# An attention and gated-MLP kernel: the first MLP product of batch 0 is split by pairs of heads, and the early pairs get offsets of their own

## The chip, the cores and the metric

The kernel runs on one core of one Trainium2 chip. Its time is the device time of one execution in microseconds (us). A run of several executions is given by its median. A profile is one execution taken by the hardware profiler; its rows count microseconds from the first instruction. The engines are called TensorE (PE in the rows; PEld is its loading of weights), VectorE (DVE), ScalarE (ACT), GpSimd (POOL) and SyncE (SP, here only a queue of transfers).

## The reference

Eight batches, eight heads, 576 positions, 64 columns per head. All in float32:

```python
q_rot, k_rot = rotate(q), rotate(k)                   # rotary embedding
scores = scale * q_rot @ k_rot.T                      # per head, 576 x 576
attn = exp(scores - max) / (sum + 1e-09)
x = (attn @ v) with the heads side by side            # 576 x 512 per batch
h = maximum(x @ w_in, 0)                              # 512 -> 1024
u, v = h[..., :512], h[..., 512:]
v_n = (v - mean(v)) / sqrt(var(v) + 1e-6)
v_s = einsum('ts,bsd->btd', w_spatial, v_n) + b_spatial[:, None]
out = (u * v_s) @ w_out                               # 512 -> 512
```

## The kernel before

Work goes by pairs of heads: pair i is two heads of batch i // 4, 32 pairs in all. For a pair, `prepare` loads q and k, multiplies them with the rotary table and adds (tiles st, on GpSimd and in part on VectorE or TensorE), and splits the results in a high part that TensorE takes at full rate and a low remainder (hq and lq for q, lk for k). From pair 4 on the parts are copied by transfers into qs, ks and qz, of which there is one each. `attention` makes nine tiles of scores (sc; tile 8 serves both heads and stands fifth), and for each the negative maximum (nmx, VectorE), the exponential (e, ScalarE) and a transposed copy (tu, VectorE); then the product with v (pv, in three chunks), and `normalise` (x, with a high and a low part). Scores have two PSUM slots, so a score waits for the exponential two scores back.

After four pairs `mlp` does the batch's MLP: pa (the half of w_in that is normalised, 5 tiles of rows, each a contraction over the four pairs' x), pb (the other half), pc (the spatial product) and pd (w_out). Each is a sum of three products of high and low parts: high by high, low by high, high by low. `norm` makes vn out of pa (vv, statistics sm, a high part on ScalarE and a remainder on GpSimd). The weights are decoded early (wi, wo: instructions on VectorE, ScalarE and GpSimd), and the spatial weights split (wsp).

Nothing is issued in the order of the code. Every operation is put into a list with a key, and `Program.run` plays the whole kernel through with its own costs and issues, for each engine, the ready operation with the lowest key whose buffers are free. Keys are 20 per pair and 80 per batch plus offsets (the tables PREP, STAGE, NORM, DEC, K at the head of the file), so a table's number moves operations before or behind others. On the chip each engine runs its list strictly in order. Where TensorE would have nothing ready early in the kernel, `run` issues warm matmuls: products of zeros of 256 columns into a free PSUM buffer.

In `rows`, the first pa of a batch waits for x of all four pairs, high and low:

```python
ahead = [*[(x[n], j) for n in range(4) for j in range(2)], *[f"wi1{n}" for n in range(4)]] if d == 0 else []
```

Of the kernel before, what the change touches and what calls it, by code (L numbers as in the profile page):

```python
# [22 lines left out]
HF = DFF // 2  # L23
# [17 lines left out]
MOE_START, MOE_LENGTH = 94.478379, 78.548222  # L41
DEC_V = [97.949631, 82.361107, 593.702782, 288.768656]
DEC_S = [84.682668, 152.53349, 99.527247]
DEC_U = [-568.813081, -65.866382, -0.431134, 175.381419]
DEC_ON = -60.279479
# [5 lines left out]
K_V = [27.234326, 64.747493]  # L51
DEC_O = [113.18323, -246.5008, -70.36556, -68.947851]
# [19 lines left out]
EARLY = -540.962515  # L72
STEAL = 253.677474
WARM_FROM, WARM_FULL, WARM_TO, WARM_NS, WARM_AFTER, WARM_COLS = 2500, 44958.22, 200000, 125, -0.15, 256
PATIENT = (DVE, ACT, POOL)
K_LATE = 163.209501
UNTIL = -5282.532269
LATE_LOAD = 300
SOON = 108.92456
FIRST = 6  # L80
PREP = [-848.367164, -374.753764, -69.9844, -244.721214, -617.60192, -1064.500205, 581.882473, -475.784363]
PREP_E = [51.687636, 298.661164, 17.879536, 140.254064, -184.884171, 639.680467, 73.636456, 484.33577]
PREP_AT = [-441.032351, -69.597063, -819.530327, -30.251418, -111.190708, 107.347515]
STAGE = [-7.255147, 1.255075, -127.272341, -353.119135, 244.349862, 3.682899, 10.320485]
STAGE_E = [-17.885167, 1.413295, -324.778667, -335.590414, -18.444203, 500.740646, 14.840595]
ATT_AT = [-7.442792, -9.232278, -6.449832, 1.846545, -111.323694, -67.478676]
NORM = [-413.12016, 513.410815, -713.32848, 231.181969, -280.547004]
NORM_E = [-178.78421, 267.172514, -208.498036, -240.944501, -239.600932]
MOE0 = [106.701094, 81.129356]
K_NORM, K_RELU, K_GATE, K_GHI, K_GLO, K_OB, K_OUT = 249.262822, 5.067081, 431.336369, -272.695754, 347.344605, 449.209189, 337.36198  # L90
# [216 lines left out]
def tile_attention_gated_mlp(  # L307
# [132 lines left out]
    def decode(key, where, at, src, after=()):  # L440

        n = f"w{'io'[where is wout]}" + "".join(map(str, at))
        tiles = {}
# [666 lines left out]
```

## Time and profile before

| | |
|---|---|
| median of 3 runs | 897.56 us (893.99 to 898.61) |
| the profiled execution | 891.51 us, its span 889.7 us |
| mean granted TensorE clock | 0.992 |
| TensorE busy | 858.7 us, 97% of the span |
| VectorE, ScalarE, GpSimd busy | 580.6, 497.5, 511.2 us |
| TensorE's share of the chain that ended last | 65%, of it warm matmuls 4% of the span |

A busy TensorE is not one that does useful work: warm matmuls count as busy. A wait is shown with the row of the instruction that ended it, as the idle time before it and the instruction (or transfer) that came last before it started.

### The profile page before, as it was taken

To read this page: it belongs to the slowest core of one execution; us is meant where nothing else is said; L and a number is where in the kernel's file an instruction comes from. 1 tells how busy PE (TensorE), PEld (TensorE's weight loads), DVE (VectorE), ACT (ScalarE), POOL (GpSimd) and SP (SyncE) were. 2 spreads that over 40 slices of the span, in tenths; PEclk is the share of its full clock that TensorE was granted. 3 is DMA by queue.
4 is the path that set the end of the run, shared out by engine and by line. 5 is a ranking of instruction groups with operands and counts; after the bars stand their busy time and mean duration, and the time that the engine had idled before them with its cause. 6 is when DMAs were issued, how large, how long until landed. Compare 5 with 4: busy or idle time off the path is not lost.

```text
span 889.7 us, 32677 instructions
## 1 busy us (share of the span) xinstructions
PE 858.7 (97%) x13709; PEld 757.9 (85%) x13709; DVE 580.6 (65%) x1169; ACT 497.5 (56%) x1239; POOL 511.2 (57%) x509
## 2 busy tenths in 40 slices
PE   9999989988999999999999999999999999999998
PEld 7666668878878998889979988899978998899898
DVE  6787788747577665857678565857687665855120
ACT  2665578635448545754558445755567555753442
POOL 7666699766357665566457664566557664312121
PEclk9998899999999999999999999999999999999999
DMA  9977646778888888877888788878987888552101
GB/s 195 246 231 188 146 104 150 174 166 190 211 175 187 189 182 213 190 175 173 210 204 193 171 179 211 186 173 187 224 200 176 187 197 205 121 115 53 54 1 55
DMA packets 99622, 150.88 MB, mean 170 GB/s; under 512 B 30929, under 2 KB 46929, under 8 KB 99474
## 3 DMA queue, kind: packets, MB, share of 16 engines
q1 hardware_dynamic: 98962, 148.12, 71.6%
q8 instruction: 108, 1.77, 0.9%
q10 hardware_dynamic: 512, 0.66, 0.3%
q14 instruction: 40, 0.33, 0.1%
HBM read 94.24 MB, written 9.88 MB: 117 GB/s over the span
## 4 chain that ended last, share of the span: by engine, by line
PE 65%; DMA 11%; issue 9%; SPq 4%; DVE 4%; POOL 4%; ACT 2%; POOLq 0%; DVEq 0%; ACTq 0%
PE sc L750 15%; PE pv L715 11%; PE pc L915 11%; PE pb L897 9%; PE pa L874 7%; PE pd L935 5%; DMA st<-in_qk_dram 4%; PE warm L1009 4%; SPq L429 3%; DMA ks<-st 2%; POOL st L563 2%; PE pr L616 1%; DMA vr<-in_v_dram 1%; DVE tu L771 1%; DVE nmx L760 1%
## 5 line engine op out<-in xcount | busy, mean ns | idle before, releaser
L760 DVE TENSOR_REDUCE nmx<-sc 128x1 f32<-128x576 f32 x288 | 211.5, 740 | 133.5 <-PE sc L750 131.2
L761 ACT ACTIVATE e<-sc,nmx 128x576 f32<-128x576 f32 x288 | 212.5, 739 | 144.7 <-DVE nmx L760 142.5
L771 DVE STREAM_TRANSPOSE tu<-e 128x576 f32<-128x576 f32 x288 | 216.5, 762 | 17.7 <-ACT e L761 9.7
L563 POOL TENSOR_TENSOR st<-st,tab 128x576 f32<-128x576 f32 x112 | 157.8, 1429 | 58.2 <-DMA st<-in_qk_dram 43.5
L715 PE MATMUL pv<-tu,vr 32*64 32x144 f32 x9216 | 177.4, 288 | 11.2 <-issue 11.2
L715 PEld LDWEIGHTS pv<-tu,vr 32*64 32x64 f32 x9216 | 147.9, 131 | 35.8 <-issue 31.8
L750 PE MATMUL sc<-ks,qs 128*128 128x288 f32 x560 | 120.9, 305 | 10.8 <-DVE rb L826 4.3
L915 PE MATMUL pc<-wsp,vn 128*128 128x288 f32 x768 | 126.2, 299 | 0.0
L874 PE MATMUL pa<-wi,x 128*128 128x512 f32 x448 | 118.6, 396 | 0.2 <-DVE rb L825 0.2
L897 PE MATMUL pb<-x,wi 128*128 128x288 f32 x768 | 117.5, 297 | 0.9 <-ACT vv L973 0.8
L935 PE MATMUL pd<-g,wo 128*128 128x288 f32 x744 | 113.6, 297 | 0.0
L915 PEld LDWEIGHTS pc<-wsp,vn 128*128 128x128 f32 x768 | 109.6, 189 | 3.6 <-issue 3.6
L750 PEld LDWEIGHTS sc<-ks,qs 128*128 128x128 f32 x560 | 88.9, 189 | 27.3 <-ACT e L761 8.8
L897 PEld LDWEIGHTS pb<-x,wi 128*128 128x128 f32 x768 | 107.0, 188 | 5.2 <-issue 2.6
L750 PE MATMUL sc<-lk,qz 128*128 128x288 f32 x504 | 108.3, 296 | 0.4 <-issue 0.4
L435 POOL TENSOR_TENSOR vn<-vv,vn 128x512 fp32r<-128x512 f32 (+1 forms) x40 | 51.4, 1292 | 98.9 <-ACT vn L432 98.6
L935 PEld LDWEIGHTS pd<-g,wo 128*128 128x128 f32 x744 | 102.9, 188 | 3.8 <-issue 3.6
L435 POOL TENSOR_TENSOR x<-rb,x 128x64 fp32r<-128x64 f32 (+1 forms) x96 | 59.4, 652 | 79.9 <-ACT x L432 79.9
L874 PEld LDWEIGHTS pa<-wi,x 128*128 128x128 f32 x448 | 79.1, 188 | 14.7 <-issue 1.8
L435 POOL TENSOR_TENSOR g<-u,g 128x288 fp32r<-128x288 f32 x64 | 51.1, 804 | 58.2 <-ACT g L432 58.2
L578 POOL TENSOR_TENSOR st<-st 128x576 f32<-128x576 f32 x56 | 80.0, 1429 | 2.9
L750 PEld LDWEIGHTS sc<-lk,qz 128*128 128x128 f32 x504 | 81.1, 189 | 0.7 <-issue 0.7
(144 smaller groups left out, 897.3 us busy)
## 6 DMA issues: line engine op xcount, KB each, us to landing
vr<-in_v_dram SPq DMA_DIRECT2D x128, 320.0 KB, 7.3
st<-in_qk_dram SPq DMA_DIRECT2D x58, 288.0 KB, 4.9
ks<-st SPq DMA_DIRECT2D x112, 144.0 KB, 4.9
st<-in_qk_dram SPq DMA_DIRECT2D x58, 256.0 KB, 5.1
qs<-hq SPq DMA_DIRECT2D x56, 164.0 KB, 4.0
qs<-lq SPq DMA_DIRECT2D x56, 164.0 KB, 3.8
out_dram<-ob SPq DMA_DIRECT2D x31, 288.0 KB, 3.1
qz<-hq SPq DMA_DIRECT2D x28, 164.0 KB, 6.8
```

Source lines behind the costliest of these rows:

```text
L435: eng.tensor_tensor(out=lo, in0=src, in1=hi.bitcast(F32), op=ALU.subtract)
L563: f = lambda e: e.tensor_tensor(out=st[j][:, cols], in0=st[j][:, cols], in1=tab2[:, cols], op=ALU.mult)
L578: f = lambda e: e.tensor_tensor(out=st[j][:, :S], in0=st[j][:, :S], in1=st[j][:, S:2 * S], op=ALU.add)
L715: nc.tensor.matmul(outs[g][64 * a:64 * a + 64], lhsT=vr[rows, NQ * (at % 4) + at // 4, a, :], rhs=tu[rows, kb, Q4 * a:Q4 * a + Q4], start= ...
L750: nc.tensor.matmul(pt[:, n_c * 512:n_c * 512 + HALF], lhsT=lhsT, rhs=rhs[:, n_c * HALF:n_c * HALF + HALF], start=(n == 0), stop=(n == len( ...
L760: op(DVE, 749, key + k_max, lambda: nc.vector.tensor_reduce(out=nmx.tile, in_=tops(pt), op=ALU.max, axis=AX.XY, negate=True), r=[pt], w=[n ...
L761: op(ACT, 920, key + k_exp, lambda: nc.scalar.activation(e.tile.rearrange("p (c n) -> p c n", c=2), tops(pt), AF.Exp, bias=nmx.tile, scale ...
L771: nc.vector.transpose(out=dst, in_=src)
L874: nc.tensor.matmul(pm[:, :HF], lhsT=lhsT, rhs=win[1, d][:, j, :], start=(d == 0 and n == 0), stop=(d == 3 and n == len(todo) - 1))
L897: nc.tensor.matmul(pm[:, :HALF], lhsT=win[0, d][:, i, f * P:(f + 1) * P], rhs=x[d][:, at:at + HALF], start=(d == 0 and n == 0), stop=(d == ...
L915: nc.tensor.matmul(pm[:, :HALF], lhsT=lhsT, rhs=rhs, start=(t == 0 and n == 0), stop=(t == 4 and n == 1))
L935: nc.tensor.matmul(pm[:, :HALF], lhsT=wout[d,][:, i, m * P:(m + 1) * P], rhs=gs[d][:, at:at + HALF], start=(d == 0 and n == 0), stop=(d == ...
```

## The change

In `rows`, for batch 0 alone, the first pa no longer waits for all x but for pair 3's token "go", which its first chunk of values sets; each pa then waits for the x of its own pair. For the fourth pair the contraction is cut in two: the two products with the high part of x and w_in's high and low parts ahead, the one with the low part of x behind, in a waiting of its own. The order of the three products is now high by high, high by low, low by high, in all batches. Early pairs (0 to 5) get one table each where they shared one, the decoding of w_in and w_out gets three offsets (DEC_G) for one, the MLP of batch 0 its own seven offsets (MOE_K0). All numbers are new. `decode`, `gate` and the others change only in which table they read.

```diff
-MOE_START, MOE_LENGTH = 94.478379, 78.548222
+MOE_START, MOE_LENGTH = 94.744184, 78.284423
...
-DEC_ON = -60.279479
+DEC_G = [-57.440314, -97.226709, 110.690024]
...
-PREP_E = [51.687636, 298.661164, 17.879536, 140.254064, -184.884171, 639.680467, 73.636456, 484.33577]
+PREP_0 = [-32.849775, 182.765619, 92.530758, 79.045448, -339.24905, 965.001318, 114.863923, 396.495195]
...
+        on = DEC_G[2 if where is wout else 1 - at[0]]
...
-        K_S, K_STEP, K_MAX, K_EXP, K_TURN, K_CHUNK, K_VAL = STAGE_E if i < FIRST else STAGE
+        K_S, K_STEP, K_MAX, K_EXP, K_TURN, K_CHUNK, K_VAL = (STAGE_0, STAGE_1, STAGE_2, STAGE_3, STAGE_4, STAGE_5)[i] if i < FIRST else STAGE
...
+        K_NORM, K_RELU, K_GATE, K_GHI, K_GLO, K_OB, K_OUT = MOE_K if b else MOE_K0
...
-                ahead = [*[(x[n], j) for n in range(4) for j in range(2)], *[f"wi1{n}" for n in range(4)]] if d == 0 else []
-
-                def mul(d=d):
-                    todo = products(x[d], t)
-                    for n, (lhsT, j) in enumerate(todo):
-                        nc.tensor.matmul(pm[:, :HF], lhsT=lhsT, rhs=win[1, d][:, j, :], start=(d == 0 and n == 0), stop=(d == 3 and n == len(todo) - 1))
-
-                key = mm(pe_ns(HF) * (2 if t == 4 else 3), mul, r=[f"wi1{d}", (x[d], 0), (x[d], 1), *ahead], w=[pm], new=[pm] if d == 0 else [])
+                ahead = [*([(x[n], j) for n in range(4) for j in range(2)] if b else [("go", NP - 1)]), *[f"wi1{n}" for n in range(4)]] if d == 0 else []
+
+                todo = [0, 1] if t == 4 else [0, 2, 1]
+                split = b == 0 and d == 3 and t < 4
+                for part in [todo[:2], todo[2:]] if split else [todo]:
+
+                    def mul(d=d, part=part, end=todo[-1]):
+                        each = products(x[d], t)
+                        for n in part:
+                            lhsT, j = each[n]
+                            nc.tensor.matmul(pm[:, :HF], lhsT=lhsT, rhs=win[1, d][:, j, :], start=(d == 0 and n == 0), stop=(d == 3 and n == end))
+
+                    low = [(x[d], 1)] if not split or part[0] == 1 else []
+                    key = mm(pe_ns(HF) * len(part), mul, r=[f"wi1{d}", (x[d], 0), *low, *ahead], w=[pm], new=[pm] if d == 0 else [])
```

What this does to the orders, at the places that the prediction speaks of. Names carry the pair or batch and the tile: sc4_8 is tile 8 of pair 4's scores, pa0_1 tile 1 of batch 0's pa, x3 pair 3's x, wi10 the decoded weights of its first 128 rows.

TensorE before, from the ninth tile of pair 4's scores (sc4_8, the fifth in order) to the first pa; sixteen warm matmuls stand ahead of it, six more ahead of sc4_2, and four between sc4_4 and pa0_0:

```order
L750 MATMUL sc4_8_2064<-ks_71,qs_70 128x288 x4
L750 MATMUL sc4_8_2064<-lk4_1314,qz_72 128x288 x2
L750 MATMUL sc4_4_2074<-ks_71,qs_70 128x288 x2
L750 MATMUL sc4_4_2074<-lk4_1314,qz_72 128x288 x2
L1009 LDWEIGHTS zero_64
L1009 MATMUL warm_2081<-zero_64 128x256
```

TensorE now, from pair 4's second score to its tile 8:

```order
L767 MATMUL sc4_1_1955<-ks_71,qs_70 128x288 x2
L767 MATMUL sc4_1_1955<-lk4_1314,qz_72 128x288 x2
L897 MATMUL pa0_0_1969<-wi10_685,x0_996 128x512 x3
L897 MATMUL pa0_0_1969<-wi11_754,x1_1349 128x512 x3
L897 MATMUL pa0_0_1969<-wi12_1047,x2_1668 128x512 x3
L767 MATMUL sc4_2_2000<-ks_71,qs_70 128x288 x2
L767 MATMUL sc4_2_2000<-lk4_1314,qz_72 128x288 x2
L767 MATMUL sc4_3_2007<-ks_71,qs_70 128x288 x2
L767 MATMUL sc4_3_2007<-lk4_1314,qz_72 128x288 x2
L897 MATMUL pa0_0_1969<-wi13_954,x3_1996 128x512 x2
L897 MATMUL pa0_1_2021<-wi10_685,x0_996 128x512 x3
L897 MATMUL pa0_1_2021<-wi11_754,x1_1349 128x512 x3
```

All 26 warm matmuls between sc4_1 and pa0_0 are gone, and 17 matmuls of pa0_0 and pa0_1 stand ahead of sc4_8; the last of pa0_0, with x3's low part, stands behind sc4_8.

GpSimd before, up to the low half of q of pairs 6 and 7 (lq made out of st6_0 and st7_0):

```order
L435 TENSOR_TENSOR wo0_2515<-vlwo0_2480,wo0_2515 128x512
L435 TENSOR_TENSOR vn_1965<-vv0_2_2350,vn_1965 128x512
L563 TENSOR_TENSOR st7_1_2271<-st7_1_2271,tab2_63 128x576 x2
L435 TENSOR_TENSOR lq_74<-st6_0_1693,hq_73 128x512
L435 TENSOR_TENSOR lq_74<-st6_0_1693,hq_73 128x4x16
L578 TENSOR_TENSOR st7_1_2271<-st7_1_2271 128x576
L435 TENSOR_TENSOR lq_74<-st7_0_1971,hq_73 128x512
```

GpSimd now, at the same place:

```order
L451 TENSOR_TENSOR wo0_2506<-vlwo0_2461,wo0_2506 128x512
L580 TENSOR_TENSOR st7_1_2194<-st7_1_2194,tab2_63 128x576
L451 TENSOR_TENSOR vn_1977<-vv0_3_2209,vn_1977 128x512
L595 TENSOR_TENSOR st7_1_2194<-st7_1_2194 128x576
L451 TENSOR_TENSOR lq_74<-st6_0_1691,hq_73 128x512
L451 TENSOR_TENSOR lq_74<-st6_0_1691,hq_73 128x4x16
L451 TENSOR_TENSOR vn_1977<-vv0_4_2428,vn_1977 64x512
L451 TENSOR_TENSOR lq_74<-st7_0_1961,hq_73 128x512
```

The remainder of vn's tile 3 (of vv0_3) and the sum of st7_1 now stand ahead of pair 6's lq; that of tile 4 stands between the two lq.

ScalarE before, at pair 6's exponentials (e6_4 is that of tile 4) and the step st8_1, the high part of pair 8's k:

```order
L761 ACTIVATE e6_8_2980,sums0_66<-sc6_8_2946,nmx6_8_2971 128x576
L900 ACTIVATE u0_3_2963<-pb0_31_2916 128x288
L652 ACTIVATE st8_1_2789<-st8_1_2789 128x576
L761 ACTIVATE e6_4_3006,sums0_66<-sc6_4_2973,nmx6_4_2990 128x576
L761 ACTIVATE e6_5_3021,sums0_66<-sc6_5_2999,nmx6_5_3011 128x576
L761 ACTIVATE e6_6_3042,sums0_66<-sc6_6_3023,nmx6_6_3031 128x576
```

ScalarE now:

```order
L924 ACTIVATE u0_3_2901<-pb0_31_2851 128x288
L778 ACTIVATE e6_8_2932,sums0_66<-sc6_8_2904,nmx6_8_2917 128x576
L778 ACTIVATE e6_4_2952,sums0_66<-sc6_4_2926,nmx6_4_2937 128x576
L778 ACTIVATE e6_5_2967,sums0_66<-sc6_5_2946,nmx6_5_2958 128x576
L669 ACTIVATE st8_1_2766<-st8_1_2766 128x576
L448 ACTIVATE g0_0_2991<-u0_0_2516 128x288
L778 ACTIVATE e6_6_2994,sums0_66<-sc6_6_2969,nmx6_6_2979 128x576
```

st8_1 has moved behind the exponentials of tiles 4 and 5, and a step of g (of the gate) stands ahead of that of tile 6.

## Rows read from the trace of the kernel before

**Rows 1.** The page: busy time of each engine, share, instructions.

```profile
PE 858.7 (97%) x13709; PEld 757.9 (85%) x13709; DVE 580.6 (65%) x1169; ACT 497.5 (56%) x1239; POOL 511.2 (57%) x509
```

**Rows 2.** Stretches: length; busy PE, PEld, DVE, ACT, POOL; clock, DMA share, GB/s.

```profile
112.00:130.00 18.00, 15.56 (x262) 11.75 (x246) 15.79 (x27) 13.05 (x30) 16.48 (x17) 1.00 0.47 112
130.00:180.00 50.00, 48.04 (x827) 42.50 (x825) 41.07 (x89) 35.20 (x89) 44.97 (x41) 1.00 0.70 155
180.00:230.00 50.00, 41.74 (x779) 38.30 (x780) 27.99 (x51) 22.46 (x56) 32.86 (x31) 0.97 0.77 175
```

**Rows 3.** Timeline of TensorE, pair 4's scores: start, length, instructions.

```profile
119.53 1.91 PE L1009 MATMUL warm<-zero 128*128 128x256 bf16 x6
121.33 0.53 PE L750 MATMUL sc<-ks,qs 128*128 128x288 f32 x2
...
122.49 2.68 PE L1009 MATMUL warm<-zero 128*128 128x256 bf16 x16
124.92 0.77 PE L750 MATMUL sc<-ks,qs 128*128 128x288 f32 x4
...
126.33 0.61 PE L1009 MATMUL warm<-zero 128*128 128x256 bf16 x4
126.78 2.35 PE L874 MATMUL pa<-wi,x 128*128 128x512 f32 x9
```

**Rows 4.** Timeline of TensorE, pairs 5 to 8; in brackets idle time and releaser.

```profile
154.57 4.56 PE L897 MATMUL pb<-x,wi 128*128 128x288 f32 x33
159.06 1.22 PE L715 MATMUL pv<-tu,vr 32*64 32x144 f32 x60
...
164.24 0.51 PE L750 MATMUL sc<-ks,qs 128*128 128x288 f32 x2 [0.71 <-DMA qs<-lq]
...
168.37 0.53 PE L750 MATMUL sc<-ks,qs 128*128 128x288 f32 x2 [0.96 <-ACT e L761]
...
182.32 0.85 PE L750 MATMUL sc<-ks,qs 128*128 128x288 f32 x2 [2.35 <-ACT e L761]
...
187.49 0.42 PE L750 MATMUL sc<-ks,qs 128*128 128x288 f32 x2
...
209.45 0.43 PE L750 MATMUL sc<-ks,qs 128*128 128x288 f32 x2
...
212.70 0.50 PE L750 MATMUL sc<-ks,qs 128*128 128x288 f32 x2 [1.48 <-ACT sums L781]
```

**Rows 5.** Timeline of GpSimd around the low halves of q.

```profile
119.15 1.65 POOL L386 MEMSET vn<- 64x512 f32 x3 [1.35 <-PE pv L715]
...
158.48 1.65 POOL L435 TENSOR_TENSOR lq<-st,hq 128x512 fp32r<-128x512 f32 x2
160.00 1.50 POOL L578 TENSOR_TENSOR st<-st 128x576 f32<-128x576 f32 x1
165.05 1.57 POOL L435 TENSOR_TENSOR lq<-st,hq 128x512 fp32r<-128x512 f32 x2 [3.55 <-DMA qs<-lq]
166.64 2.62 POOL L435 TENSOR_TENSOR vn<-vv,vn 128x512 fp32r<-128x512 f32 x2
```

**Rows 6.** Timeline of VectorE: lk of pairs 6 and 7.

```profile
159.12 2.99 DVE L540 SCALAR_TENSOR_TENSOR lk<-st 128x576 fp32r<-128x576 f32 x1
...
164.32 0.76 DVE L540 SCALAR_TENSOR_TENSOR lk<-st 128x576 fp32r<-128x576 f32 x1
```

**Rows 7.** Timeline of ScalarE: st8, the exponential behind it, pair 7's last.

```profile
180.86 0.68 ACT L652 ACTIVATE st<-st 128x576 fp32r<-128x576 f32 x1 [2.97 <-POOL st L578]
181.45 0.72 ACT L761 ACTIVATE e<-sc,nmx 128x576 f32<-128x576 f32 x1
...
211.13 0.74 ACT L761 ACTIVATE e<-sc,nmx 128x576 f32<-128x576 f32 x1 [0.28 <-DVE nmx L760]
```

**Rows 8.** Stretches as in rows 2, behind the wait of 2.35.

```profile
182.00:184.00 2.00, 1.68 (x7) 1.69 (x8) 1.09 (x2) 0.99 (x4) 1.92 (x3) 0.56 1.01 224
184.00:186.00 2.00, 2.00 (x11) 2.00 (x11) 1.30 (x3) 0.83 (x2) 1.06 (x1) 0.59 0.13 34
```

More of the change, by code (lines that the diff above doesn't have):

```diff
@@ L83 @@
[L83 to L89, printed above, removed]
@@ new lines @@
+NORM = [-428.465703, 609.682147, -692.799463, 236.099243, -298.747737]
+NORM_0 = [-244.559891, 517.601008, -157.093041, -167.545156, -105.82433]
+NORM_1 = [-192.810612, 190.930437, -214.131948, -74.395379, -216.726448]
+NORM_2 = [-280.191903, 293.806751, -51.742277, -217.96091, -290.765893]
+NORM_3 = [-223.29783, 172.651756, -240.046007, -365.293658, -238.893886]
+NORM_4 = [-144.081309, 379.339015, -91.243063, -180.710848, -372.571447]
+NORM_5 = [-135.364254, 127.973129, -108.584507, -265.034273, -292.363128]
@@ L476, in decode @@
-        op(ACT, 500, key - DEC_ON, lambda: nc.scalar.activation(pt.tile, ints(), AF.Copy, bias=1.0, scale=2.0**-20), w=[pt])
-        op(DVE, 640, key - DEC_ON, lambda: stt(out=val.tile, in0=word(0, U32), scalar=2.0**-52, in1=pt.tile, op0=ALU.mult, op1=ALU.add), r=[t0, pt], w=[val], new=[val])
+        op(ACT, 600, key - on, lambda: nc.scalar.activation(ints(), ints(), AF.Relu, bias=bias, scale=float(2**23)), r=["bias"], w=[pt])
+        op(DVE, 640, key - on, lambda: stt(out=sg.tile, in0=word(1), scalar=-(2**31), in1=ints(), op0=ALU.bitwise_and, op1=ALU.bitwise_or), r=[t1, pt], w=[sg], new=[sg])
@@ L479, in product @@
+        op(DVE, 640, key - on, lambda: ts(out=ints(), in0=word(1), scalar1=0xFFFFF, scalar2=None, op0=ALU.bitwise_and), r=[t1], w=[pt])
+        op(ACT, 500, key - on, lambda: nc.scalar.activation(pt.tile, ints(), AF.Copy, bias=1.0, scale=2.0**-20), w=[pt])
+        op(DVE, 640, key - on, lambda: stt(out=val.tile, in0=word(0, U32), scalar=2.0**-52, in1=pt.tile, op0=ALU.mult, op1=ALU.add), r=[t0, pt], w=[val], new=[val])
         def product(e):
             e.tensor_tensor(out=val.tile, in0=val.tile, in1=sg.tile.bitcast(F32), op=ALU.mult)
-        prog.either({POOL: pool_ns(HF), **({DVE: 640} if key - DEC_ON < EARLY else {})}, key - DEC_ON, lambda e: product(vec[e]), r=[sg], w=[val])
@@ L483, in decode @@
-        op(ACT, 480, key - DEC_ON, high, r=[val], w=[t0, t1, (n, "hi")])
-        prog.either({POOL: pool_ns(HF), **({DVE: 640} if key - DEC_ON < EARLY else {})}, key - DEC_ON, lambda e: rest_lo(vec[e], where[at][:, 1, :], val.tile, where[at][:, 0, :]), r=[val, (n, "hi")], w=[n])
+        prog.either({POOL: pool_ns(HF), **({DVE: 640} if key - on < EARLY else {})}, key - on, lambda e: product(vec[e]), r=[sg], w=[val])
+        op(ACT, 480, key - on, high, r=[val], w=[t0, t1, (n, "hi")])
+        prog.either({POOL: pool_ns(HF), **({DVE: 640} if key - on < EARLY else {})}, key - on, lambda e: rest_lo(vec[e], where[at][:, 1, :], val.tile, where[at][:, 0, :]), r=[val, (n, "hi")], w=[n])
@@ L994, in norm, with gate @@
             op(POOL, pool_ns(HF), key, port=True, f=lambda: rest_lo(nc.gpsimd, vn(4, 0)[64:P], vv[0:64], vn(4, 0)[0:64]), r=[vv, ("vn", t, 0)], w=[("vn", t, 1)])
-    def gate(u, g, c, pm, key, done):
+    def gate(u, g, c, pm, key, done, ks):
+        K_GATE, K_GHI, K_GLO = ks
         cc = slice(c * HALF, (c + 1) * HALF)
```

53 lines of the change are left out of this document (33 added, 20 removed).

## The prediction

> **What bounds the kernel now.** I read the page first: TensorE is busy 97% of the span [rows 1], so the end moves only by what TensorE does for nothing or waits for. Then the table by stretch [rows 2], to see where that is: of the 50 us from 180 on it is busy 41.74, and in the 18 us before 130 it has 2.44 us idle, and part of the busy time there is warm matmuls on zeros, which give no result. In the stretch 130 to 180 the picture is another: VectorE 41.07, GpSimd 44.97 of 50, so a TensorE that gets ahead there may only wait longer. Third, the timeline of TensorE between the scores of pair 4 [rows 3]: three runs of warm matmuls lie there, 6, 16 and 4, after which the first MLP product starts at 126.78. Fourth, the same timeline up to pair 8 [rows 4], for the waits that come next: 0.71 ahead of pair 6's first score, 0.96 ahead of its second, 2.35 ahead of its eighth (tile 6), 1.48 ahead of pair 8's first. Last, GpSimd [rows 5], VectorE's lk [rows 6] and ScalarE [rows 7] around those waits, for what ends them, and the granted clock behind the longest [rows 8].
>
> Up to the scores of pair 3 all engines' orders are as before but for neighbours changing places, and from pair 11 on TensorE executes the same work ahead of each score again; the sum is therefore made between 104 and 230 us. After that TensorE is the bound, and I carry the shift to the end unchanged; TensorE's whole idle time is 889.7-858.7 = 31.0 us, 12.7 of it in the three stretches of [rows 2], so swaps of neighbours behind 230 have a part of the other 18.3 to win or to double, most of it early: I take 0, and 2 either way into the range.
>
> **The change part by part.**
> *The early products.* The 26 warm matmuls go. By starts in [rows 3] they hold TensorE for 121.33-119.53 = 1.80, 124.92-122.49 = 2.43 and 126.78-126.33 = 0.45, together 4.68 us. In their place stand 17 pa matmuls at 2.35/9 = 0.26 us, 4.4 us, so the scores of pair 4 stay where they are within 0.3 us and the MLP is 4.4 to 4.7 us ahead. pa's last product of tile 0 now waits for pair 3's low half from GpSimd. It stands behind the fifth score of pair 4 in order (tile 8), near 126, and one weight remainder that stood ahead of that low half is now behind it; I take no wait (bound: 0.5, as the first pa stood at 126.78 for all of x). Queued behind that matmul are only scores and the next pa, in order.
>
> *To pair 6's first score.* Before it the new order has 18 pb matmuls more. One is (159.06-154.57)/33 = 0.136 [rows 4], so 2.45 us. TensorE would come there at 164.24-0.71-4.68+2.45 = 161.3. But that score needs the low half of q, which GpSimd makes. In the order before, GpSimd makes it at 158.48 and is done at 160.00; GpSimd has no idle time between 119.15 and there (its two ends in [rows 5]). The new order puts two more operations ahead: the remainder of vn's tile 3, 2.62/2 = 1.31, and the sum of st7, 1.50. Against that GpSimd may use part of its 1.35 idle at 119.15, since the operation now first there is a decode product, whose input the order of VectorE has two instructions sooner, and not the zeroing of vn that waited for TensorE's values: between 0 and 1.35, I take 1.0, nearer the upper end, as two VectorE instructions are worth about that. So the low half is done at 160.00+1.31+1.50-1.0 = 161.81. From there to the score it took 164.24-160.00 = 4.24 (two copies on the SP queue and their landing; nothing is moved ahead of them on SP there). The score starts at 166.05, and TensorE waits 4.75 in place of 0.71. Of the lead of 4.68, only 2.45-1.81 = 0.64 is left here.
>
> *From there to pair 6's eighth score.* Before: 182.32-164.24 = 18.08, with 0.96 and 2.35 of waits, so 14.77 of work. Now 18 pb fewer and 2 pc more, -16 x 0.136 = -2.18: 12.59. The 0.96 goes because ScalarE has fewer vv and vn steps ahead of pair 6's first exponential (the vv and vn of the MLP's tile 3 are done before it). The 2.35 goes because ScalarE no longer stands at st8 (idle 2.97 until GpSimd's sum, [rows 7]) ahead of exponentials 4 and 5; st8 is now behind them. What is late next is exponentials 6 and 7 behind st8, which hold pair 7's first score. GpSimd's sum for st8 ended at 180.86 [rows 7]; it moves by the low half's 1.81, less the vn remainder that now stands ahead of the low half, 1.31, plus one st9 product that is new ahead of it, 1.5 as the sum in [rows 5]: 182.9 at the latest. With ScalarE's st8 (181.45-180.86 = 0.59), one g and the exponential, some 1.9 together, the slot is free at 184.8, just before the score wants it (185.0 below). The cost of the long wait: after the 2.35 idle the granted clock was 0.56 and 0.59, the lower level of 1.2 GHz in most of 4 us [rows 8], which cost 1.68x0.44+2.00x0.41 = 1.56 us. After 1.48 [rows 4] it did not fall: the stretch 180 to 230 as a whole has 0.97 [rows 2], which those 4 us explain. A wait of 4.75 is over 2.35, so I take the fall, 1.56; without it the gain is that much larger. Pair 6's eighth score: 166.05+12.59+1.56 = 180.20.
>
> *To pair 7's first score.* Before 187.49-182.32 = 5.17 with those 1.56 in it; now 9 pc more, 1.22: 4.83, at 185.03. By then 11 more pc are done, 1.50. Lead: 187.49-185.03+1.50 = 3.96.
>
> *To pair 8.* Four warm matmuls are new between the pc there, 4 x 2.43/16 = 0.61. Ahead of pair 8's first score, 16 pc stand behind pair 7's last (209.45) in place of 8, 1.09 us more cover for a wait of 1.48 [rows 4]. Against that the values of pair 7 now follow directly on that score, and need its last exponential (211.13 [rows 7], 1.68 behind the score, 0.74 long, and VectorE's transposed copy behind it, put at as much; TensorE has 16 x 0.136 and two scores in that time, about 3): some 0.5 us of wait. Net 0.6 gained.
>
> Sum: 3.96-0.61+0.6 = 4.0 us. The sum is against the profiled execution, 891.51 us (span 889.7), so 887.5; the median of the runs shown is 897.56, 0.7% above it, and I take the same 4.0 from it: 893.5.
>
> **A rule weighed.** VectorE's lk of pair 6 took 2.99 us at 159.12 and the next one, 164.32, 0.76 [rows 6]; GpSimd worked without a break beside the first and was idle from 161.5 to 165.05 before the second [rows 5]. The Trainium skill, SBUF — State Buffer, "Who interferes with whom", says that a VectorE instruction with two inputs in SBUF and a GpSimd instruction that reads SBUF exclude one another for a whole instruction, and that the order of issue decides who blocks. The trace agrees: lk ended when GpSimd paused. By that rule the new order, which puts a vn remainder into that pause, speaks against the change.
>
> **The rivals.**
> *Slower: GpSimd's unbroken stretch now outlasts TensorE's lead.* The place is pair 6's first score. Nothing of the 1.35 is recovered (1.0 lost against my sum), pair 7's lk also meets a busy GpSimd (2.99-0.76 = 2.23 during which VectorE takes no maximum of pair 6), and exponentials 6 and 7 stand 2.35 behind st8 as 4 and 5 did, with a second fall of the clock, 1.56. 4.0-1.0-2.23-2.35-1.56 = -3.1: 900.7. For it: GpSimd's 44.97 of 50. Against it: in the order VectorE has nothing urgent at that lk. The rule weighed above is this mechanism's. It decides from the point where pair 6's first score starts later than 164.24+2.45 = 166.7; I forecast 166.05.
> *No change: the lead is eaten at pair 6 and not given back.* If the wait at the eighth score only moves to the ninth or to pair 7, the 0.64 left at pair 6's first score less the 0.61 of warm matmuls remain: 897.5. For it: pairs 6 and 7 need VectorE and ScalarE for each score. Against it: both are busy 28.0 and 22.5 of 50 us from 180 on [rows 2].
> *All of it kept.* If the low half is not later than before (the planner has put vn's remainder where GpSimd would have waited), TensorE keeps the 4.68, loses the waits of 0.96 and 2.35 and the 1.56 of low clock, and the last two terms cancel: 9.5, or 888.0. For it: the idle 3.55 of GpSimd right behind [rows 5]. Against it: two operations stand ahead of it in the order, whatever follows.
>
> **How the numbers follow.** Mine 0.50 (890.5 to 896.0: without the fall of the clock 5.5 gained, with 1.35 recovered 0.35 more; with 0 recovered and a wait behind st8 1.5 left). All kept 0.15 (888 to 890.5). No change 0.20 (896 to 898.5). Slower 0.15 (899 to 902). The range that leaves out half of the best case and most of the slower one is 888.5 to 899. A measurement of this kernel can tell 0.5%, 4.5 us, from no change: the line lies at 893.1, inside my own case. Faster takes a little over half of mine and all of "all kept", 0.42; slower only the far end of the slower case, 0.07; within, 0.51.
>
> **What would show it.** Right: pa starts before pair 4's third score, no run of warm matmuls behind 112, a wait of 3 to 5 us ahead of pair 6's first score with a granted clock near 0.5 behind it, no wait over 1 us at pair 6's eighth score, and TensorE's busy time less by 4 to 5. Wrong: that wait under 1 us (the gain is then near 9), or the first score of pair 6 later than 166.7, or new waits over 1 us in 230 to 890, where I price nothing.

## The result, and the profile after

The kernel after takes 901.36 us (median of 15 runs, 894.84 to 909.64), the kernel before 895.2 (15 runs, 887.12 to 900.76): a ratio of 1.0091, interval 1.0065 to 1.0117. The ratios in this text are formed from the fast executions of both kernels, so they are not the quotients of the medians (1.0069 here). It is slower, where I forecast 893.5 and gave slower a chance of 0.07. The profiled executions are 904.19 us (span 902.3) and 891.51.

The page of after, first its busy row (columns as in [rows 1]), then the group with the most idle time on TensorE: busy, mean ns, then idle time and what ended most of it.

```profile
PE 860.0 (95%) x13686; PEld 761.6 (84%) x13686; DVE 578.0 (64%) x1169; ACT 498.4 (55%) x1239; POOL 513.1 (57%) x509
L767 PE MATMUL sc<-ks,qs 128*128 128x288 f32 x560 | 121.2, 306 | 20.1 <-DVE rb L843 12.4
```

The same group in the kernel before:

```profile
L750 PE MATMUL sc<-ks,qs 128*128 128x288 f32 x560 | 120.9, 305 | 10.8 <-DVE rb L826 4.3
```

TensorE's work is the same within 1.3 us [rows 1]; what grew is idle time, and most of it is scores that wait for rb, the normaliser's sums. These go by SP to DRAM and back, turned (rt, rtNd, rb), and VectorE scales a pair's values with them; a following score waits for the PSUM that this frees.

The last two stretches of [rows 2], of after, and one more, 230 to 330, with before's row of it last:

```profile
130.00:180.00 50.00, 43.19 (x788) 38.71 (x787) 37.30 (x87) 33.73 (x86) 45.40 (x41) 0.97 0.67 149
180.00:230.00 50.00, 44.84 (x817) 41.05 (x816) 34.03 (x62) 24.90 (x62) 33.25 (x32) 1.00 0.86 190
230.00:330.00 100.00, 92.53 (x1617) 83.55 (x1616) 62.29 (x133) 54.99 (x139) 56.84 (x55) 1.00 0.77 180
```

```profile
230.00:330.00 100.00, 97.30 (x1655) 88.05 (x1654) 68.45 (x143) 56.93 (x146) 58.46 (x56) 1.00 0.84 189
```

The gain at 180 to 230 (44.84 in place of 41.74 busy) is there, and it is paid back on both sides: 4.85 at 130 to 180 and 4.77 at 230 to 330. Both losses are new waits; the second lies where I priced nothing.

The lines that answer to [rows 3, 4], TensorE of after:

```profile
121.75 2.21 PE L897 MATMUL pa<-wi,x 128*128 128x512 f32 x9
...
167.06 0.50 PE L767 MATMUL sc<-ks,qs 128*128 128x288 f32 x2 [0.66 <-DMA qs<-lq]
...
175.22 0.54 PE L767 MATMUL sc<-ks,qs 128*128 128x288 f32 x2 [3.35 <-DVE rb L843]
...
190.18 0.51 PE L767 MATMUL sc<-ks,qs 128*128 128x288 f32 x2 [0.81 <-issue]
...
247.64 2.96 PE L959 MATMUL pd<-g,wo 128*128 128x288 f32 x21
...
282.57 0.77 PE L767 MATMUL sc<-ks,qs 128*128 128x288 f32 x4 [2.95 <-DVE rb L843]
```

The first product runs early, as the change says. Pair 6's first score waits 0.66, not the 4.75 that I forecast; its third score waits 3.35, for rb of pair 5. Pair 7 starts at 190.18 (185.03 forecast, 187.49 before).

To place the loss I took the start of each pair's first and last maximum on VectorE from both traces. After is behind before by 1.70 us at pair 4's first, 3.55 at pair 5's last, 2.75 at pair 6's first, 1.60 at pair 8's first, 4.97 at pair 12's last, and 12.64 at pair 31's last. The 1.70 I count as chance: TensorE's granted clock was at the lower level (0.5, 1.2 GHz) from 83.45 to 97.11 in after and from 83.24 to 93.48 in before, 3.42 us longer, of which half is lost; another profile of the same order up to there (after with more instructions, below) had 10.24 us of it. That it is chance alone is not shown: the four profiles with before's early order had 10.24 each. So in these two profiles the early part has brought 0.1 us by pair 8 in place of 4, pairs 8 to 12 cost 3.4, and the rest 7.7, of which two falls of the clock (3.41 us long each, at 609 and 711, half of that lost) are 3.4.

After's profile is a good one of its early order, as the profiles of the experiments below show. From pair 4's first maximum to pair 8's first it took 97.3 us; the nine profiles with this order there took 97.3 to 103.0 (mean 99.9), the four with before's 95.8 to 98.6 (mean 97.1). The ranges overlap, but in the mean the early part costs 2.8 us where I forecast a gain of 4.

### The profile page after: what moved, and what is told of

Read it like the earlier page. It is cut to its first block, busy times and chain, and to the rows that moved or that the text cites. A ratio compares the mean times of both kernels' runs of the same rounds, so it can differ in the third digit from the quotient of the medians.

```text
span 902.3 us, 32617 instructions
## 1 busy us (share of the span) xinstructions
PE 860.0 (95%) x13686; PEld 761.6 (84%) x13686; DVE 578.0 (64%) x1169; ACT 498.4 (55%) x1239; POOL 513.1 (57%) x509
## 4 chain that ended last, share of the span: by engine, by line
PE 63%; DMA 13%; SPq 8%; issue 6%; DVE 4%; POOL 3%; ACT 2%; ACTq 0%; DVEq 0%; POOLq 0%
PE sc L767 15%; PE pc L939 11%; PE pv L732 11%; PE pb L921 9%; PE pa L897 8%; PE pd L959 7%; SPq L445 5%; DMA st<-in_qk_dram 3%; DMA vr<-in_v_dram 2%; PE warm L1034 2%; DMA qz<-hq 1%; DVE tu L788 1%; DMA qs<-lq 1%; PE pr L633 1%; POOL st L580 1%
## 5 line engine op out<-in xcount | busy, mean ns | idle before, releaser
L732 PE MATMUL pv<-tu,vr 32*64 32x144 f32 x9216 | 179.1, 289 | 13.7 <-issue 12.9
L767 PE MATMUL sc<-ks,qs 128*128 128x288 f32 x560 | 121.2, 306 | 20.1 <-DVE rb L843 12.4
L939 PE MATMUL pc<-wsp,vn 128*128 128x288 f32 x768 | 128.3, 301 | 1.0 <-DVE nmx L777 1.0
L921 PE MATMUL pb<-x,wi 128*128 128x288 f32 x768 | 120.6, 299 | 0.3
L897 PE MATMUL pa<-wi,x 128*128 128x512 f32 x448 | 116.4, 395 | 0.0
```

The lines of the kernel that those rows point to most:

```text
L732: nc.tensor.matmul(outs[g][64 * a:64 * a + 64], lhsT=vr[rows, NQ * (at % 4) + at // 4, a, :], rhs=tu[rows, kb, Q4 * a:Q4 * a + Q4], start= ...
L767: nc.tensor.matmul(pt[:, n_c * 512:n_c * 512 + HALF], lhsT=lhsT, rhs=rhs[:, n_c * HALF:n_c * HALF + HALF], start=(n == 0), stop=(n == len( ...
L897: nc.tensor.matmul(pm[:, :HF], lhsT=lhsT, rhs=win[1, d][:, j, :], start=(d == 0 and n == 0), stop=(d == 3 and n == end))
L921: nc.tensor.matmul(pm[:, :HALF], lhsT=win[0, d][:, i, f * P:(f + 1) * P], rhs=x[d][:, at:at + HALF], start=(d == 0 and n == 0), stop=(d == ...
L939: nc.tensor.matmul(pm[:, :HALF], lhsT=lhsT, rhs=rhs, start=(t == 0 and n == 0), stop=(t == 4 and n == 1))
```

## The experiments

Before is run beside each group. Each ratio is of a kernel against before, with its 95% interval. The early theories were A (the structure itself), B (the normaliser's trip on SP), C (the count of instructions on TensorE), D (the new numbers of the tables for later pairs); later ones R (SP's order of the normaliser's fetches), W (TensorE's own order) and X (the late end of batch 0's MLP keeps x of pair 7 out, that keeps the one rb buffer, and the normalisers of pairs 8 and 9 are late).

### Structure, count and tables

**The structure alone**, in before with its own tables:

```diff
+ahead = [("go", NP - 1)] if b == 0 else [...]     # pa's waits
+for part in [[0, 2], [1]] if b == 0 and d == 3 else [...]
```

> The kernel before, with every number of its tables as it was, and only the two edits of the first MLP step: the wait for the fourth pair's value step in place of the four x tiles, and the fourth pair's multiplies in two parts. In its order, as in the kernel after, pair 9's normaliser goes out and comes back on SP behind the next pair's st loads, and 26 warm-up multiplies are gone. A, the structure costs the time by itself: 901 us (ratio to before 1.006 to 1.009). B, the place of the normaliser's round trip on SP costs it: 899 to 901, with one idle of 2 to 3 us on TensorE before pair 10's scores, released by VectorE's rb. C, the place of the instruction count against the fetched blocks costs it: anything from 892 to 901, since this kernel has its own count (52 instructions fewer than before). D, the searched tables cost it: 892 to 895, no worse than before.

902.03 us, 1.0074 (1.0046 to 1.0102). Slower by itself, and its longest wait is one that after does not have. Its rows on VectorE and on TensorE:

```profile
145.11 5.02 DVE L540 SCALAR_TENSOR_TENSOR lk<-st 128x576 fp32r<-128x576 f32 x1
151.76 0.85 PE L750 MATMUL sc<-ks,qs 128*128 128x288 f32 x2 [8.60 <-DVE rb L826]
```

lk takes 5.02 us where it took 2.99 and 0.76 [rows 6], the scaling by rb stands behind it on VectorE, and TensorE waits 8.60. GpSimd's five instructions from 142.94 to 149.52, all with inputs in SBUF, follow on one another there without a break. The Trainium skill, SBUF — State Buffer, "Who interferes with whom", says that the port pair that VectorE shares with GpSimd is an exclusive lock, and that a VectorE instruction with two SBUF inputs contends with a GpSimd instruction that reads SBUF. The trace agrees: lk ends at 150.13, 0.61 behind the last of these five. In after, with all its new tables, the same lk takes 1.95. Behind pair 8 this kernel loses as after does, with before's tables: x of pair 7 on ScalarE starts at 251.35, behind a wait of 4.12 for pd, and the score at 286.16 waits 2.31 for rb.

**After with more instructions**: 23 pa multiplies issued as two of 256 columns. **Before with fewer**: the last 46 warm matmuls as 23 of 512 columns.

```diff
-nc.tensor.matmul(pm[:, :HF], lhsT=lhsT, rhs=win[1, d][:, j, :], ...)
+for lo, hi in ((0, 256), (256, 512)):             # for 23 of them
+    nc.tensor.matmul(pm[:, lo:hi], lhsT=lhsT, rhs=win[1, d][:, j, lo:hi], ...)
```

```diff
+cols = 256 if n < 231 else 512 if n % 2 else 0    # of the n-th warm matmul
```

> The kernel after, with its order untouched, and 23 of the first multiplies of the MLP's first step (512 columns) issued as two of 256, so that from pair 7 on each of TensorE's instructions has the number that it has in the kernel before (46 instructions more than after). C, the instruction count decides where TensorE runs out of fetched instructions in the value steps: 894 to 897 us, 4 to 7 below the kernel after, idle before pv put down to issue back from 12.9 to about 11 us, and the clock falls at 609 and 711 us gone. A, B and D: 901 us as the kernel after, within 1.5.

> The kernel before, with its order untouched, and the last 46 warm-up multiplies of 256 columns issued as 23 of 512, so that each of TensorE's instructions after them has the number that it has in the kernel after (46 fewer than before). C: 899 to 901 us, ratio to before 1.004 to 1.007, idle before pv put down to issue up by 1.5 to 2 us and clock falls behind 500 us. A, B and D: as before, 895 us within 1.5 (ratio 0.998 to 1.002).

The first 907.47, 1.015 (1.0114 to 1.0186); the second 894.82, 1.0018 (0.9995 to 1.004). The count as it was before makes after no faster, and the count of after makes before no slower: C falls. The first is 6 us above after, which none of the theories said; the cause is open. The idle time put down to issue ahead of pv does move with such edits (12.9 us in after, 18.6 and 9.4 in these two, 11.2 in before), but the time doesn't follow it.

**After with before's numbers in the tables of pairs from 6 on and of the MLP from batch 1 on:**

```diff
-PREP, STAGE, NORM, MOE_START, MOE_LENGTH, K_V[1], MOE_K = (after's)
+PREP, STAGE, NORM, MOE_START, MOE_LENGTH, K_V[1], MOE_K = (before's)
```

> The kernel after, with the tables for pairs 6 to 31 and for the MLPs of batches 1 to 7 as they were before (the two edits and all early tables as after). Its order has the normalisers of pairs 8 and 9 ahead of the st loads on SP, as before. A, the structure or the early tables cost the time: 900 to 902. B, the normaliser's round trip: 896 to 898, the idle of 2.95 us before pair 10's scores gone, and no clock fall behind 500 us only by chance. C, the instruction count (48 fewer than before): 900 to 902. D, the late tables as a whole: 894 to 896.

903.63, 1.013 (1.0087 to 1.0174). It told little, since pairs 6 and 7 no longer fit the early tables: lk took 6.12 us there, again beside a GpSimd without a break, a score waited 8.23 behind it, and that covers whatever came later.

```profile
153.36 6.12 DVE L557 SCALAR_TENSOR_TENSOR lk<-st 128x576 fp32r<-128x576 f32 x1
```

### The late normalisers of pairs 8 and 9

What stands behind the 2.95 at 282.57, in after: x of pair 7 on ScalarE and GpSimd, the fetch of pair 8's rb on SP, then pair 9's, and its scaling on VectorE.

```profile
248.64 0.78 ACT L448 ACTIVATE x<-rb 128x512 fp32r<-128x512 f32 x2 [2.42 <-PE pd L959]
249.35 1.85 POOL L451 TENSOR_TENSOR x<-rb,x 128x512 fp32r<-128x512 f32 x3 [2.21 <-ACT x L448]
251.54 1.94 SPq L445 DMA_DIRECT2D rb<-rt8d  x3
274.92 1.92 SPq L445 DMA_DIRECT2D rb<-rt9d  x3
281.54 0.52 DVE L842 TENSOR_TENSOR rb<-pv,rb 128x144 f32<-128x144 f32 x2 [3.38 <-DMA rb<-rt9d]
```

And in before x of pair 7 (GpSimd's part; ScalarE's began at 241.92, not 248.64), the fetch of pair 8's rb, and its scaling:

```profile
242.62 1.84 POOL L435 TENSOR_TENSOR x<-rb,x 128x512 fp32r<-128x512 f32 x3 [15.05 <-ACT x L432]
244.49 2.74 SPq L429 DMA_DIRECT2D rb<-rt8d  x3
251.44 0.52 DVE L825 TENSOR_TENSOR rb<-pv,rb 128x144 f32<-128x144 f32 x2 [1.02 <-DMA rb<-rt8d]
```

There is one rb. It is free when x of pair 7 has been read out of it (244.46 before, 251.20 after), and rb of pair 8 is fetched then: 244.49 and 251.54. From that issue to the scaling it is 6.95 us in before (251.44 - 244.49) and 7.72 in after (at 259.26). And x of pair 7 is late because it waits for pd, w_out's product of batch 0: in after no pd stands ahead of pair 7's values and 72 of 96 ahead of pair 8's, where before has 24 and 84. The structure alone, with before's tables, has 0 and 72 as well and the same late x of pair 7 (251.35), so this comes without the new numbers.

**SP's order alone.** The fetches that stand behind other transfers in after are put ahead of them; then also pair 5's; and in before, pair 8's and 9's are held behind the loads:

```diff
+HOLD = {"st12_0": "rb8", "vr9": "rb8", "ob0_3": "rb8", "st12_1": "rt9", "st13_0": "rb9"}   # after: held until
+HOLD = {..., "st8_0": "rb5"}                                                              # after, second
+HOLD = {"rb8": "vr9", "rt9": "st12_1", "rb9": "st13_0"}                                   # before
```

> The kernel after; every engine's order as it was but SP's, where five moves change places so that they stand as in the kernel before: rb of pair 8 ahead of st12_0, vr9 and the fourth output tile, rt of pair 9 ahead of st12_1, rb of pair 9 ahead of st13_0. R, the normalisers of pairs 8 and 9 come late because SP issues other loads first: VectorE's scale of pair 8 at about 252 to 254 us in place of 259, no idle of 2.95 us before pair 10's scores, the 6 us that pairs 9 and 10 take longer than before are gone, 896 to 898 us (4 to 6 below the kernel after). W, the 6 us come from TensorE's own order there: 900 to 902, the waits only change their names.

> As the kernel with pairs 8 and 9 first, and also rb of pair 5 ahead of st8_0 (three issues of 0.6 us). R: rb of pair 5 issued 1.9 to 2 us sooner, the idle of 3.35 us before pair 6's third score 1.2 to 2 us, perhaps too short for the clock to fall (1.7 us more): 2 to 3.5 us below the kernel with pairs 8 and 9 alone, 893 to 896 us. W: 900 to 902.

> The kernel before; every engine's order as it was but SP's, where rb of pair 8 is put behind st12_0 and vr9, rt of pair 9 behind st12_1 and rb of pair 9 behind st13_0, as in the kernel after. R: VectorE's scale of pair 8 later by 4 us or more, an idle of 2 to 3 us on TensorE before pair 10's scores released by VectorE's rb, 3 to 6 us in all: 897 to 900 us, ratio to before 1.003 to 1.007. W: 894 to 895, as before.

907.33, 1.0138 (1.0094 to 1.0181); 909.66, 1.0151 (1.0103 to 1.02); 909.17, 1.0156 (1.0117 to 1.0195). R falls as a cure: ahead in the queue, the fetch holds SP until x of pair 7 leaves rb. SP's and GpSimd's rows of the first:

```profile
245.76 0.54 SPq L455 DMA_DIRECT2D out_dram<-ob  x1
...
253.39 1.85 POOL L461 TENSOR_TENSOR x<-rb,x 128x512 fp32r<-128x512 f32 x3 [2.08 <-ACT x L458]
255.27 1.92 SPq L455 DMA_DIRECT2D rb<-rt8d  x3
```

From 246.30 to 255.27 SP does nothing, and loads stand behind it. The third says that the lateness is enough by itself: in before, with the fetch at 252.03, TensorE waits 9.59 us at one place.

```profile
252.03 1.92 SPq L439 DMA_DIRECT2D rb<-rt8d  x3
...
261.33 1.62 PE L884 MATMUL pa<-wi,x 128*128 128x512 f32 x3 [9.59 <-DVE rb L835]
```

**The trip of pair 5 taken away**: `SPREAD = 5` is the first pair whose sums go by DRAM.

```diff
-SPREAD = 5
+SPREAD = 6
```

> The kernel after with pair 5's normaliser spread by TensorE, as those of pairs 0 to 4 are (one constant, 5 to 6): 32 narrow multiplies on ones in place of the trip to DRAM and back. The planner writes its order anew with it; rt and rb of pair 9 come to stand ahead of the st loads, rb of pair 8 does not. R: the idle of 3.35 us before pair 6's third score and the clock fall behind it are gone for about 0.5 us of multiplies, and the idle of 2.95 us before pair 10's scores: 4 to 8 us below the kernel after, 893 to 897 us. W: the time moves with TensorE's order, and could be 898 to 904.

905.49, 1.0113 (1.0078 to 1.0148). It is no gain: another order of the whole early part comes of it, and what it did to the wait alone can't be told.

**The cause taken away** (X against R and W): the last 12 pd of batch 0 get a key that is lower by 200.

```diff
+sooner = 200 if b == 0 and m == 3 and c == 1 else 0    # of pd's key
```

> The kernel after; the planner's key of the last output group of batch 0's MLP (12 multiplies of pd) lowered by 200. In the order all 96 multiplies of pd then stand ahead of pair 8's values on TensorE (before: 84 and 12 inside; after: 72, and 21 of the rest behind pair 9's third score), SP's rt and rb of pair 9 come to stand ahead of the st loads by themselves, and from pair 11 on all is as in the kernel after. X, the late end of that MLP keeps the slot that pair 7's x needs, x keeps the one rb buffer, and so the normalisers of pairs 8 and 9 come late: x of pair 7 on ScalarE at about 242 us in place of 248.6, the scale of pair 8 at about 252 in place of 259.3, the idle of 2.95 us before pair 10's scores gone, 4 to 6 us below the kernel after, 895 to 898 us. Y, what is lost is lost elsewhere (the late tables, pair 5): 900 to 902.

```profile
242.63 0.76 ACT L448 ACTIVATE x<-rb 128x512 fp32r<-128x512 f32 x2
...
251.65 1.91 SPq L445 DMA_DIRECT2D rb<-rt8d  x3
```

901.36, 1.0079 (1.0044 to 1.0114), beside 901.36 of after: no gain in the median. The mechanism goes most of the way: x of pair 7 is at 242.63, and the fetches of pair 9 move ahead of the loads by themselves, but rb of pair 8 is still issued at 251.65, behind a load. TensorE's waits from 230 on, in after (to 341) and here (to 340), as "engine line, what it waited for: us, times, longest":

```profile
PE pv L732 <- issue: 3.3, 3, 1.7
PE sc L767 <- DVE rb L843: 2.9, 1, 2.9
PE sc L767 <- DMA qs<-lq: 1.0, 1, 1.0
```

```profile
PE pv L732 <- issue: 1.8, 3, 1.1
PE sc L767 <- DVE rb L843: 1.6, 1, 1.6
```

7.2 has become 3.4, where before has 2.7. From pair 8's first maximum to pair 12's last it took 121.9 us, before 121.8 and after 125.1. Over the profiles: five with after's order there took 125.1 to 128.7 (mean 127.2), three with before's 121.4 to 121.8 (121.6), three with these pd ahead 121.9 to 123.8 (122.6). So after's order costs some 5.6 us there, and this edit gives 4.7 of it back.

The profile loses it again ahead of that, by three more falls of the clock (at 190, 200 and 217). Each comes with a wait of TensorE: 1.81 at pair 7's first score (189.12), 2.44 in pair 7's values (199.78, put down to issue), 2.00 at pair 8's first score (216.97). In after the same three places waited 0.81, 1.35 and 0.93, with no fall. Five of the nine profiles with this early order have falls between 189 and 225, none of the four with before's. With the late tables of before, the same edit is worth 2 to 3 us in the medians, below.

### The late tables

Before's numbers from pair 12 and batch 3 on in after; after's numbers there in before; the first with the twelve pd ahead as well:

```diff
+LATE = 12
+... = STAGE_L if i >= LATE else STAGE      # so PREP, NORM, K_V; MOE_L, MOE_KL from batch 3
```

> The kernel after up to pair 11, and from pair 12 and the third batch's MLP on with the tables of the kernel before. D, the late tables cost 3 to 5 us between pair 12 and the end (in the runs so far that stretch took 476 to 482 us in five kernels with the late tables of after, 470 to 477 in five with those of before): 896 to 899 us. X, nothing is lost there but by chance: 900 to 902.

> The kernel before up to pair 11, and from pair 12 and the third batch's MLP on with the tables of the kernel after. D: 3 to 5 us above the kernel before, 897 to 900 us, ratio 1.003 to 1.006, the stretch from pair 12 to the end 476 to 480 us. X: as before, 893 to 896.

> The kernel after with both changes: the last output group of batch 0's MLP ahead of pair 8's values, and from pair 12 on the tables of the kernel before. X and D both right: 890 to 894 us, no slower than the kernel before. X alone: 895 to 898. D alone: 896 to 899. Neither: 900 to 902.

897.49, 1.0042 (1.0011 to 1.0072); 895.28, 1.001 (0.9981 to 1.0038); 894.24, 0.9984 (0.9957 to 1.001). So taking the late tables back alone is worth 3.9 of the 6.2 us, taking back pd's late end alone nothing in the median, and the two together all of it. Whether the numbers are bad as such is open: in before they cost 0.1%, but the interval reaches 0.4%, as much as in after. From pair 12's last maximum to pair 31's last, the seven profiles with after's numbers took 475.0 to 481.9 (mean 477.8), the seven with before's 469.7 to 476.8 (mean 472.5). TensorE's waits in that stretch, before and then after:

```profile
PE sc L750 <- DVE rb L826: 4.0, 5, 1.0
PE pv L715 <- issue: 3.2, 5, 1.2
PE sc L750 <- ACT e L761: 0.5, 2, 0.3
PE sc L750 <- issue: 0.4, 1, 0.4
```

```profile
PE pv L732 <- issue: 5.7, 5, 1.8
PE sc L767 <- DVE rb L843: 5.3, 6, 1.4
PE sc L767 <- ACT e L778: 1.3, 1, 1.3
PE sc L767 <- issue: 0.7, 1, 0.7
```

No one wait carries it; the sum of many goes from 8.1 to 13.0.

**Which table**: the MLP's alone; the pairs' alone; the pairs' with the twelve pd ahead; of the pairs' only STAGE (the scores').

```diff
+MOE_L, MOE_KL from batch 3                      # first
+PREP_L, STAGE_L, NORM_L, K_V from pair 12       # second; third: and sooner = 200
+STAGE_L from pair 12                            # fourth
```

> The kernel after; from the third batch's MLP on the MLP's tables as before, those of the pairs as after. If the MLP's late tables carry the loss behind pair 12 (the groups of pb in another order, the output of the first group one place earlier on SP): 896 to 899 us as with all late tables. If those of the pairs carry it: 900 to 902.

> The kernel after; from pair 12 on the tables of the pairs (preparation, scores, normaliser) as before, those of the MLP as after. If those of the pairs carry the loss behind pair 12: 896 to 899 us. If the MLP's carry it: 900 to 902. If neither k1 nor k2 is below 900, it takes both, or the loss is not the tables'.

> The kernel after, from pair 12 on with the tables of the pairs as before, and the last output group of batch 0's MLP ahead of pair 8's values. X (the late end of that MLP costs pairs 9 and 10 what they take longer): 3 to 5 us below the kernel with the pairs' late tables alone (897.97), 893 to 895 us. If what pairs 9 and 10 give back is lost again ahead of them, as in the kernel with the last output group alone: 897 to 899.

> The kernel after, from pair 12 on with the table of the scores alone as before (when a score, its maximum, exponent and transposes are due): TensorE's order is that of the kernel with all the pairs' late tables, SP's that of the kernel after. If the order of TensorE and VectorE in the steady batches carries the loss: 897 to 899 us. If it was the loads of pairs 11 and 12 in the other order: 900 to 903.

904.6, 1.0128 (1.0082 to 1.0174); 897.97, 1.0055 (1.0024 to 1.0087); 895.73, 0.9998 (0.9973 to 1.0023); 900.1, 1.0068 (1.0037 to 1.0099). By the medians it is the pairs' tables, not the MLP's, but the profiles don't bear that out: from pair 12's last maximum to pair 31's last the first took 472.9 us, as short as with before's numbers, and the other three 471.3 to 471.8. The first lost ahead of that stretch (pair 12's last maximum starts at 349.32, in after at 340.23), where its order is that of after. So in these single profiles either table is enough to shorten the stretch, and which one the median loss hangs on stays open. The fourth has the order of the second on TensorE and VectorE and SP's of after. Its median lies between them with overlapping intervals, but its stretch (471.3) is as short as the second's (471.8): the loads of pairs 11 and 12, which change places on SP in the second, are not needed for that.

### The early wait for pair 5's normaliser

On top of the version with both undone: pair 5's fetch held ahead of a load; and 16 matmuls on zeros put into the batch's first pb of tile 3, ahead of the waiting score.

```diff
+HOLD = {"st8_0": "rb5"}
```

```diff
+for _ in range(16):
+    nc.tensor.matmul(pm[:, HALF:HALF + 224], lhsT=zero[:, :P], rhs=zero[:, :224], start=False, stop=False)
```

> The kernel with both changes (last output group ahead, late tables of before), and rb of pair 5 ahead of st8_0 on SP, nothing else moved. If the trip of pair 5's normaliser sets pair 6's third score: the wait of 2.45 us there 0.5 to 1.2 us, no clock fall at 171 us, 1 to 3 us below the kernel with both, 891 to 893 us, and so 0.2 to 0.4% below the kernel before. If it is hidden anyway (the next wait takes its place): 893 to 895.

> The kernel with both changes, and 16 warm-up multiplies of 224 columns on zeros (some 1.5 us) on TensorE ahead of pair 6's third score, where it waits 2 to 3.4 us; they add zeros to columns that nothing reads. If the clock fall behind that wait costs 1.7 us and the warm-up keeps the clock up: 1 to 2 us below the kernel with both, 892 to 893. If the fall comes anyway or is as rare as in the kernel before: 893 to 896, no gain.

896.49, 1.0026 (0.9993 to 1.0058); 898.87, 1.0045 (1.0013 to 1.0078), beside 894.24 without. First the version without, then these two:

```profile
171.12 0.85 PE L773 MATMUL sc<-ks,qs 128*128 128x288 f32 x2 [2.45 <-DVE rb L849]
...
186.86 0.51 PE L773 MATMUL sc<-ks,qs 128*128 128x288 f32 x2 [1.62 <-ACT g L454]
```

```profile
171.59 0.53 PE L783 MATMUL sc<-ks,qs 128*128 128x288 f32 x2 [1.15 <-DVE rb L859]
...
189.26 0.64 PE L783 MATMUL sc<-ks,qs 128*128 128x288 f32 x2 [5.04 <-DMA qs<-lq]
```

```profile
175.18 0.53 PE L773 MATMUL sc<-ks,qs 128*128 128x288 f32 x2 [0.84 <-DVE rb L849]
...
190.68 0.51 PE L773 MATMUL sc<-ks,qs 128*128 128x288 f32 x2 [2.86 <-DMA qs<-lq]
```

In the first the wait is halved, in the second it is covered, and in neither does a fall of the clock follow it. Pair 7's first score then waits for its own q, 5.04 and 2.86: what TensorE gained it lost to the preparation of q.

No version was measurably faster than before: the two best lie at 0.9984 and 0.9998.

## Why the prediction was wrong

*The products fit in place of the warm matmuls: right.* pa runs at 0.25 us each (2.21/9), ahead of pair 4's tile 8, and no wait came there; GpSimd's order didn't hold it.

*"The score starts at 166.05, and TensorE waits 4.75 in place of 0.71": wrong on TensorE's side.* The score started at 167.06, so q came 1.0 late to my forecast. But TensorE came at 167.06 - 0.66 = 166.40 and not at 161.3. Of these 5.1, 1.7 is the early clock and 2.5 are new waits between 121 and 166, a stretch that I took to be without them (0.9 I can't place):

```profile
PE sc L767 <- ACT e L778: 2.0, 2, 1.3
PE pv L732 <- ACT vv L997: 0.8, 1, 0.8
```

against 0.3 in before. TensorE had the multiplies, but ScalarE had not made the exponentials sooner.

*"The 0.96 goes ... the 2.35 goes": right, but a wait that I didn't see takes their place.* Between the start of pair 5's values and pair 6's third score, before had 30 multiplies of pb and after has 15; with the wait of 0.96, which is gone, they were the cover of pair 5's trip through DRAM. That trip in after, on VectorE and SP:

```profile
161.89 0.15 DVE L854 STREAM_TRANSPOSE rt<-sums 128x32 f32<-128x32 f32 x1
162.25 1.95 DVE L557 SCALAR_TENSOR_TENSOR lk<-st 128x576 fp32r<-128x576 f32 x1
174.28 0.52 DVE L842 TENSOR_TENSOR rb<-pv,rb 128x144 f32<-128x144 f32 x2 [5.65 <-DMA rb<-rt5d]
```

```profile
162.07 0.35 SPq L445 DMA_DIRECT2D rt5d<-rt  x1
164.40 1.43 SPq L445 DMA_DIRECT2D qs<-lq  x2
167.86 1.91 SPq L445 DMA_DIRECT2D rb<-rt5d  x3
```

It is 12.4 us from transpose to scaling, with q's copies and a load ahead of the fetch. In before it was 13.3 (158.34 to 171.68) with the same ahead of it, but there the scaling came only behind pair 5's last values, and no score waited for it. The score waits 3.35, and the clock falls behind it, as it did behind the 2.35 of before [rows 8]:

```profile
175.00:177.00 2.00, 1.78 (x9) 0.65 1.10 224
177.00:179.00 2.00, 2.00 (x10) 0.50 1.09 233
```

So the fall of 1.56 that I priced happened, at another score. My lead of 3.96 at pair 7's first score measured 2.69 us late, of which 1.7 is the early clock. So the term failed by its overlap: I let TensorE's lead stand where the exponentials, the trip through DRAM and q set the time. The rival "no change: the lead is eaten at pair 6 and not given back" is near to what this part did in after's profile, and too kind to it in the mean of nine (2.8 us lost); the two kernels of the last group show no gain by mending that wait.

*"I take 0, and 2 either way" behind 230: the step that decided.* In the two profiles it is 3.4 us up to pair 12 and 7.7 behind, in the means of the profiles 5.6 and 5.3; in the medians the two edits that undo it are together worth 5.6 to 7.1 (901.36 to 895.73 and 894.24), about three times the bound that I gave it. I argued that from pair 11 on TensorE executes the same work ahead of each score, and that it is the bound. The first was read too coarsely: in most batches nine multiplies of pb (1.2 us) that stood ahead of a score stand behind it in after. And neither bounds a wait: the order behind pair 8 differs in where the last pd stand, and on the late tables' neighbours hang waits of about 1 us each, many times over. The warning stood in my own text as a sign of failure (new waits over 1 us behind 230), yet not in the range.

*The rival "slower" was wrong in its place.* Pair 7's lk did not decide in after. Its mechanism is real: it made the structure alone slower (lk 5.02 us), where the tables didn't move lk.

The sum, by what the runs show: the early products bring nothing that can be measured (0.9984 and 0.9998 with the rest undone); taking back the late tables is worth 3.4 to 3.9 us (901.36 to 897.97 and 897.49), and pd's late end 2.2 to 3.3 on top (897.97 to 895.73, 897.49 to 894.24). Together they undo the loss of 6.2 us in the medians. The means of the profiles add up to more (2.8, 5.6 and 5.3); they are few single executions, and the sizes are rough. For pd the rows show how; for the tables they show only that many waits grow, and since each table alone writes a new order, luck with an order is not excluded there. Of the 12.6 us that the profiled execution lost, 5.1 are lower clock at 83 to 97, 609 and 711.

## What to carry to other kernels

Work that is moved ahead leaves a gap where it stood: ask first which transfer it was hiding there. Where one buffer hands work from one stage to the next (here rb, held by x of pair 7 until the last pd), follow it past the end of the edit, since a late end reaches the next batch by it. When a change brings a new order for everything, the far stages have to be priced one by one like the edited one, and where that can't be done the range must say so.

## What the runs showed of the hardware

The granted clock didn't follow the length of the wait alone: with a wait of 1.81 us in one kernel (to 189.12, pd ahead) and of 2.45 in another (to 171.12, both undone) it fell to 0.5 for 3.4 us, with 2.95 in after (to 282.57) it stayed at 1.00. An lk of 128x576 took 0.76, 1.95, 2.99, 5.02 and 6.12 us in these traces; it was shortest where GpSimd was idle, and longest beside a GpSimd that worked without a break. A fetch from DRAM (rb of pair 8 in before), issued after SP had issued nothing for 1.90 us, took 6.95 us to the start of the instruction that waited for it. SP stood still for 8.97 us (246.30 to 255.27) behind one fetch that waited for its buffer, with loads behind it that after issues ahead of that fetch.
